# First batch's scores with tokens in the partitions, softmax along the free dimension, weights turned back by TensorE; both x halves from SyncE, activation table asked for early

## The chip, the cores and the metric

The kernel runs on one core of a Trainium2 chip. The metric is the device time of one execution in microseconds. Before the change three runs took 664.93, 666.25 and 666.53 us; the median, 666.25 us, is what the changed kernel is compared with. The trace comes from one more execution, whose own time was 665.42 us.

## The reference

There are 8 batches of 512 tokens in 8 heads of 64 numbers, and for each batch and head a state of 32 rows. The state reads the tokens and the tokens read the state (two softmax attentions over the same scores), and both results, laid side by side as 8 x 544 rows of 512, go through a two-layer network with an activation that is 0 below -1, the input above 1 and a parabola between.

```python
scores = scale * np.matmul(x, state.transpose(0, 1, 3, 2))     # B,H,512,32
a = softmax over the 32;   xread = np.matmul(a, state)
scores2 = scale * np.matmul(state, x.transpose(0, 1, 3, 2))    # B,H,32,512
a2 = softmax over the 512; sread = np.matmul(a2, x)
h = concatenate([xread, sread]).reshape(4352, 512) @ w_in      # 512 x 2048
g = np.where(h >= 1, h, np.where(h <= -1, 0.0, (h + 1) ** 2 / 4))
out = g @ w_out                                                 # 2048 x 512
```

All is float32. `x` is 26.7 times as large as drawn, so the softmaxes are far from flat.

## The kernel before, in words

Batches run one after the other, and each batch runs through 8 steps j, each with 256 of the 2048 columns of the hidden layer. Two heads and a state row block are joined into one contraction of 128 (4 pairs of heads with 32 state rows), so that the tokens' attention weights multiply a product of state and `w_in` directly: `sw` = state x `w_in` chunk, then `h` = `sw` x attention weights, then the activation, then `acc` += g x `w_out` chunk. Every large product is done as three float32r products of high and low parts (`ath`/`atl` for the weights of attention, `sw_h`/`sw_l`, `gh`/`gl`, `wo` high and low). Half of the work of VectorE (DVE) and ScalarE (ACT) is to make these parts.

The weights come in an encoded form: each chunk of `w_in` (`raw_i`) and of `w_out` (`raw_o`), 1 MB each, is decoded by three operations of 128x1024: `low` (on ACT or DVE), `high` (ACT) and `join` (DVE, L595); a `w_out` chunk is then also split (`part_high` on ACT, L602, `part_low` on DVE, L606). That decoding of 8 + 8 chunks happens once, during batch 0.

The start of the program and all of batch 0 are therefore ordered by a planner (`Plan`): each operation is given an engine, a cost, its prerequisites and the buffers that it takes and ends. The planner simulates a list schedule by rank (the length of the chain behind an operation, plus a hand-set `BIAS` for 19 operations), and emits the instructions in the order of that schedule. On PE (TensorE) and SP (SyncE, which issues the loads) the order is that of the listing. Where the plan leaves PE idle between the first scores and the first `g2`, `emit` fills in matmuls of the identity into a scratch tile (`warmed`, L198), one for each 0.34 us that the plan sees free. They do no work for the result.

Batch 0's attention, in the order of its steps, per q (the two heads of each pair, q = 0 and 1):

- `scores` (L253): state is the stationary operand (64x32), tokens move; the result `sc` has the 128 (pair, state row) in partitions and 512 tokens along the free dimension. For batch 0 it is done in two halves of 256 tokens, as the two halves of `xt` arrive. The first half of `xt` is issued by SP, the second by ACT.
- `turn` (L260): DVE transposes blocks of 32x32, so that the 32 state rows of a head lie along the free dimension (`z`); four half turns.
- `top1` (L271), `less1` (L275), `exp1` (L280, ACT), `sum1` (L284), `inv1` (L288, L289), `norm1` (L293): the softmax over 32.
- `back` (L300): DVE turns the weights back into `zt`; `high1` (L303, ACT) and `rest` (L306, DVE) split them into `ath` and `atl`.
- `top2` (L318, L319) and `exp2` (L322, ACT): the maximum and the exponential over the 512 tokens, from `sc` as it stands. `turn2` (`e2p`, L333), `keep_turned`, `read2` (`sr`, L350), `scale2`, `keep2` (`rt`) and `keep` finish the state's read.

PE's order is: fills, scores half 0, scores half 1, `sw` of chunk 0, h of step 0 (12 matmuls, L475 to L477), `sw` of chunk 1, then for each step j from 1: h of step j, `sw` of chunk j+1, the first half of `g2` of step j-1 (12 matmuls, L533 to L535), one item of the table `between`, the second half of `g2`. `e2p` of batch 0 is the item of j = 0. `sw`, `e2p`, `sr`, `sc` of batch 1 and `rt` share one pair of PSUM banks, `mm`, with one buffer; the scores of batch 0 and `acc` share `acc`, with four. `h` has two buffers, freed by `bound` (L487). The buffer of `xt` is single: batch 1's load, which stands on SP ahead of `raw_i` 3 and `raw_o` 2, waits until batch 0's scores are through.

After batch 0 (from `steps` on, L788) the order is written out by hand and nothing of the weights is left to decode.

Of the kernel before, what the change touches and what calls it, by code (L numbers as in the profile page):

```python
# [18 lines left out]
PAD = 120  # L19
BIAS = {('square', 0, 7): 4.9, ('high', 'o', 5): 4.6, ('wol', 7): -5.5, ('back', 0, 1): 2.8, ('atl', 1, 0): -6.5, ('w', 1): -2.8, ('swh', 0, 4): 4.5, ('wol', 5): 9.6, ('top2', 1, 1): 2.5, ('woh', 5): 4.1, ('swl', 1, 0): -0.5, ('swl', 0, 7): 2.1, ('gh', 0, 7): 0.6, ('low', 'i', 0): 2.6, ('wol', 6): 4.0, ('back', 1, 0): -2.1, ('turn', 0, 0, 1): -8.6, ('bound', 1, 0, 0): 3.3, ('high', 'o', 0): -4.3}  # L20

# [116 lines left out]
def state_exchange_moe(  # L138
# [39 lines left out]
    def ps_acc(name):  # L178
        return ps.tile([P, DM], F32, tag="acc", bufs=4, name=name)
# [45 lines left out]
    class Attention:  # L225
# [8 lines left out]

        def scores(self, half=None):
            b = self.b
            if half != 1:
                if b:
                    sc = ps_mm(f"sc{b}")
                    self.sc = [sc[:, hh] for hh in range(2)]  # L240
                else:
                    self.sc = [ps_acc(f"sc{b}_{hh}") for hh in range(2)]
                self.z = work.tile([P, 2, S], F32, tag="z", bufs=1, name=f"z{b}")
                self.m1 = small.tile([P, 2 * NM], F32, tag="m1", name=f"m1_{b}")
                self.s1 = small.tile([P, 2 * NM], F32, tag="s1", name=f"s1_{b}")
            for pr in range(NPR):
                for hh in range(2):
                    rows = slice(hh * 64, hh * 64 + 64)
                    o = self.sc[hh][pr * NS:(pr + 1) * NS]
                    m = self.xt[rows, :, pr]  # L250
                    if half is not None:
                        o, m = o[:, half * S // 2:(half + 1) * S // 2], m[:, half]
                    nc.tensor.matmul(o, lhsT=sb[rows, b, pr], rhs=m, start=True, stop=True)  # L253

        def tokens(self, half):
            return slice(None) if half is None else slice(half * S // 2, (half + 1) * S // 2)

        def turn(self, q, half=None):
            t = self.tokens(half)
            nc.vector.transpose(out=self.z[:, q, t], in_=self.sc[q][:, t])  # L260

# [4 lines left out]
        def top1(self, q, half=None):  # L266
            v, m, _ = self.parts(q)
            if half is not None:
                t = slice(half * NM // 2, (half + 1) * NM // 2)
                v, m = v[:, t], m[:, t]  # L270
            nc.vector.tensor_reduce(out=m, in_=v, op=ALU.max, axis=AX.X)  # L271

        def less1(self, q):
            v, m, _ = self.parts(q)
            nc.vector.tensor_tensor(  # L275
                out=v, in0=v, in1=m[:, :, None].broadcast_to([P, NM, NS]), op=ALU.subtract
            )
# [175 lines left out]
    class Hidden:  # L453
# [6 lines left out]

        def product(self, i):
# [5 lines left out]
            hp = ps_h(f"h{b}_{j}_{i}")  # L467
            for r in range(per):
                f = (2 * j + i) * per + r
                wh, wl = chunk[b, f // 2]  # L470
                sl = slice((f % 2) * P, (f % 2 + 1) * P)
                o = hp[:, r * n:(r + 1) * n]
                for k in range(nk):
# [4 lines left out]
            self.hs.append(hp)  # L478

# [160 lines left out]
    def att_start(b, half=None):  # L640
        if half != 1:
            atts[b] = Attention(b)
        atts[b].scores(half)

    def att_ops1(b):
# [27 lines left out]
    def att_ops2(b):  # L673
# [3 lines left out]
        for q in range(2):  # L677
            k = (b, q)
            take = [("tmp" if b == 0 else "e2", ("e2", b))] if q == 0 else []
            op(("top2",) + k, "DVE", 0.75, m("top2", q), [("sc", b) if b else ("sc", b, 1)] + [("top2", b, 0)] * q, take=take)  # L680
            op(("exp2",) + k, "ACT", 0.66, m("exp2", q), [("top2",) + k], ends=[("sc", b)])
# [20 lines left out]

    def product(i, b, j):
        if i == 0:
            hid[b, j] = Hidden(b, j)
        hid[b, j].product(i)

# [43 lines left out]
    op(("sc done", 0), "ACT", 0, lambda: None, [("exp2", 0, 0), ("exp2", 0, 1)])  # L751
    sw_ops(0, 0, 1)
    between = {
        0: lambda: tensor(("e2p", 0), 0.9, lambda: atts[0].turn2(), [("exp2", 0, 0), ("exp2", 0, 1)],
                          take=[("mm", ("e2p", 0))]),
        1: lambda: tensor(("sr", 0), 1.1, lambda: atts[0].read2(), [("kept", 0), ("dma", "xn", 0)],
                          take=[("mm", ("sr", 0))], ends=[("e2", 0), ("xn", 0)]),
        2: lambda: tensor(("sc", 1), 1.1, lambda: att_start(1), [("dma", "sb", 1), ("dma", "xt", 1)],
                          take=[("mm", ("sc", 1))], ends=[("xt", 1)]),
        3: lambda: tensor(("rt", 0), 0.3, lambda: atts[0].keep2(), [("rs", 0)], take=[("mm", ("rt", 0))]),  # L760
        4: lambda: tensor(("e2p", 1), 0.9, lambda: atts[1].turn2(), [("exp2", 1, 0), ("exp2", 1, 1)],
                          take=[("mm", ("e2p", 1))]),
        5: lambda: tensor(("sr", 1), 1.1, lambda: atts[1].read2(), [("kept", 1), ("dma", "xn", 1)],
                          take=[("mm", ("sr", 1))], ends=[("e2", 1), ("xn", 1)]),
        6: lambda: tensor(("rt", 1), 0.3, lambda: atts[1].keep2(), [("rs", 1)], take=[("mm", ("rt", 1))]),
    }
    for j in range(NJ):
        g1_ops(0, j)
        hidden_ops(0, j)
        if j + 1 < NC:  # L770
# [5 lines left out]
        if j == 2:  # L776
            att_ops1(1)
            att_ops2(1)
# [4 lines left out]
    with guard:  # L783
        plan.emit(warm, ("sc", 0, 0), ("g2", 0, 0, 0))

# [74 lines left out]
```

## Time and profile before

| | |
|---|---|
| median of three runs | 666.25 us |
| the profiled execution's own time | 665.42 us |
| its span, first to last instruction | 663.7 us |
| PE busy | 654.3 us (99%) |
| DVE busy | 340.0 us (51%) |
| ACT busy | 357.4 us (54%) |
| real h matmuls begin | 21.58 us |
| first `g2` matmul | 31.53 us |

PE's busy time counts the fills too, so that a busy PE in the first 28 us is not PE at useful work. The busy times of DVE and ACT are means over a stage in which they have no pause (the decoding of the weights in batch 0) and a long one in which they are half idle.

### The profile page before, as it was taken

The page shows a single profiled execution, that of the slowest core. Times are in us where ns is not written, and L with a number is a line of the kernel's source. Part 1 is how long each engine was busy: PE and PEld are TensorE (multiplying, and loading weights), DVE is VectorE, ACT ScalarE, POOL GpSimd, SP SyncE. Part 2 cuts the span into 40 slices and gives each one's busy share as a digit, 9 for nine tenths or more (in the row PEclk, how much of TensorE's full clock was granted, in tenths as well). Part 3 has the DMA queues.
Part 4 walks back from the last instruction along what each step waited for, and adds up shares of the span by engine and source line. Part 5 has one row for each costly group of instructions (what it writes and reads, how often), then busy time and mean ns, then how long its engine had stood idle before and what let it go on. Part 6 is the DMA issues. An engine that isn't in the chain of part 4 may idle for free.

```text
span 663.7 us, 10308 instructions
## 1 busy us (share of the span) xinstructions
PE 654.3 (99%) x4444; PEld 516.1 (78%) x4444; DVE 340.0 (51%) x489; ACT 357.4 (54%) x462; POOL 0.8 (0%) x7
## 2 busy tenths in 40 slices
PE   7999999999999999999999999999999999999997
PEld 6777777777777777777787777777788777778896
DVE  4999947623673338533573239433563343333531
ACT  4899847544564446544554447444653454454542
POOL 0000000000000000000000000000000000000000
PEclk9899999999999999999999999999999999999999
DMA  8896103010201003010301003010100001000101
GB/s 347 350 394 273 64 1 126 1 65 0 105 23 49 16 1 127 0 65 1 127 1 64 1 15 114 0 65 0 65 1 1 1 25 40 1 1 1 63 1 33
DMA packets 11085, 43.65 MB, mean 66 GB/s; under 512 B 1312, under 2 KB 1440, under 8 KB 7968
## 3 DMA queue, kind: packets, MB, share of 16 engines
q1 hardware_dynamic: 5952, 33.75, 13.4%
q10 hardware_dynamic: 5088, 9.24, 3.7%
q8 instruction: 35, 0.57, 0.4%
q14 instruction: 10, 0.08, 0.0%
HBM read 34.08 MB, written 8.91 MB: 65 GB/s over the span
## 4 chain that ended last, share of the span: by engine, by line
PE 92%; ACT 4%; DVE 2%; DMA 1%; issue 0%; ACTq 0%; SPq 0%
PE acc L533 19%; PE acc L534 18%; PE acc L535 18%; PE h L475 9%; PE h L476 9%; PE h L477 9%; PE sw L417 5%; DMA xt<-in_xt_dram 1%; PE sr L350 1%; PE sc L253 1%; PE e2p L333 1%; ACT u L481 1%; PE warmed L198 1%; ACT raw_i L587 1%; ACT gh L496 0%; ACT raw_o L587 0%
## 5 line engine op out<-in xcount | busy, mean ns | idle before, releaser
L533 PE MATMUL acc<-wo,gh 128*128 128x512 f32 x544 | 218.9, 402 | 0.0
L481 ACT ACTIVATE u<-h,half 128x512 f32<-128x512 f32 x136 | 93.6, 690 | 222.3 <-PE h L477 204.3
L534 PE MATMUL acc<-wo,gh 128*128 128x512 f32 x544 | 212.2, 390 | 0.0
L535 PE MATMUL acc<-wo,gl 128*128 128x512 f32 x544 | 212.2, 390 | 0.0
L487 DVE SCALAR_TENSOR_TENSOR u<-u,h 128x512 f32<-128x512 f32 x136 | 87.0, 681 | 206.4 <-ACT u L484 206.4
L533 PEld LDWEIGHTS acc<-wo,gh 128*128 128x128 f32 x544 | 102.1, 188 | 40.0 <-ACT u L481 12.8
L535 PEld LDWEIGHTS acc<-wo,gl 128*128 128x128 f32 x544 | 102.1, 188 | 22.6 <-issue 0.4
L534 PEld LDWEIGHTS acc<-wo,gh 128*128 128x128 f32 x544 | 102.3, 188 | 19.0
L501 DVE TENSOR_TENSOR gl<-u,gh 128x1024 fp32r<-128x1024 f32 x68 | 83.1, 1223 | 33.0 <-ACT gh L496 32.0
L496 ACT CAST gh<-u 128x1024 fp32r<-128x1024 f32 x68 | 71.6, 1052 | 50.8 <-DVE u L487 50.4
L484 ACT ACTIVATE u<-u 128x1024 f32<-128x1024 f32 x68 | 72.3, 1063 | 1.3
L417 PE MATMUL sw<-w,sb 64*32 64x256 f32 x1024 | 36.1, 384 | 2.2 <-DVE w L595 2.2
L417 PEld LDWEIGHTS sw<-w,sb 64*32 64x32 f32 x1024 | 15.1, 106 | 18.2 <-issue 9.5
L548 ACT COPY o<-acc 128x512 f32<-128x512 f32 x33 | 18.6, 585 | 9.1 <-PE acc L535 9.0
L476 PE MATMUL h<-ath,sw_0l 128*128 128x512 f32 x60 | 23.4, 389 | 0.0
L477 PE MATMUL h<-atl,sw_6h 128*128 128x512 f32 x60 | 23.4, 389 | 0.0
L475 PE MATMUL h<-ath,sw_0h 128*128 128x512 f32 x60 | 23.4, 392 | 0.0
L477 PE MATMUL h<-atl,sw_2h 128*128 128x512 f32 x60 | 23.4, 389 | 0.0
L477 PE MATMUL h<-atl,sw_0h 128*128 128x512 f32 x60 | 23.3, 389 | 0.0
L475 PE MATMUL h<-ath,sw_2h 128*128 128x512 f32 x60 | 23.3, 389 | 0.0
L476 PE MATMUL h<-ath,sw_2l 128*128 128x512 f32 x60 | 23.3, 389 | 0.0
L475 PE MATMUL h<-ath,sw_4h 128*128 128x512 f32 x60 | 23.3, 389 | 0.0
(173 smaller groups left out, 736.0 us busy)
## 6 DMA issues: line engine op xcount, KB each, us to landing
raw_i<-in_moe_w_in_dram SPq DMA_DIRECT2D x8, 1024.0 KB, 6.6
raw_o<-in_moe_w_out_dram SPq DMA_DIRECT2D x8, 1024.0 KB, 8.5
xn<-in_x_dram SPq DMA_DIRECT2D x8, 1024.0 KB, 5.5
out_dram<-o ACTq DMA_DIRECT2D x32, 256.0 KB, 2.0
xt<-in_xt_dram SPq DMA_DIRECT2D x15, 512.0 KB, 4.5
xt<-in_xt_dram ACTq DMA_DIRECT2D x1, 512.0 KB, 7.7
sb<-in_state_dram SPq DMA_DIRECT2D x1, 448.0 KB, 11.9
out_dram<-o SPq DMA_DIRECT2D x4, 64.0 KB, 1.7
```

The costliest lines, as they stand in the source:

```text
L417: nc.tensor.matmul(pt[pr * NS:(pr + 1) * NS, hh, i * CI:(i + 1) * CI], lhsT=sb[rows, b, pr], rhs=w32[c + i][rows, pr], start=True, stop=True,)
L475: nc.tensor.matmul(o, lhsT=wh[:, k, sl], rhs=ah[:, k], start=first, stop=False)
L476: nc.tensor.matmul(o, lhsT=wl[:, k, sl], rhs=ah[:, k], start=False, stop=False)
L477: nc.tensor.matmul(o, lhsT=wh[:, k, sl], rhs=al[:, k], start=False, stop=last)
L481: nc.scalar.activation(out=self.u[:, i], in_=self.hs[i], func=AF.Relu, scale=0.5, bias=half)
L484: nc.scalar.activation(out=self.u, in_=self.u, func=AF.Square)
L487: nc.vector.scalar_tensor_tensor(out=self.u[:, i], in0=self.u[:, i], scalar=1.0, in1=self.hs[i], op0=ALU.min, op1=ALU.max,)
L496: nc.scalar.copy(out=gh, in_=self.u)
L501: nc.vector.tensor_tensor(out=gl, in0=self.u, in1=gh.bitcast(F32), op=ALU.subtract)
L533: nc.tensor.matmul(a, lhsT=lh, rhs=oh, start=f == 0, stop=False)
L534: nc.tensor.matmul(a, lhsT=lh, rhs=ol, start=False, stop=False)
L535: nc.tensor.matmul(a, lhsT=ll, rhs=oh, start=False, stop=f == NF - 1)
```

## The change

The table `BIAS` is emptied. Both halves of batch 0's `xt` are issued by SP, one after the other. A first instruction on ACT copies one column of a scratch tile, so that the activation table is asked for before data arrive.

For batch 0, `scores_turned` computes the scores with tokens in the partitions: 64x128 of `xt` is the stationary operand and the state (64x32) moves, 16 products for each half of the tokens. `top1` and `less1` read that PSUM tile (`st`) directly, so the four half turns go. After `norm1` the weights are turned by TensorE (`turn_back`, 4 transposes of 128x128 for each q, into `zt` in `mm`) in place of DVE's `back`. `ath` and `atl` then read PSUM.

The old scores (`sc`), which `top2` and `exp2` need, are still computed, in one piece, on PE behind h of step 0; `top2` and `exp2` follow them. h of step 0 is cut in two by the contraction: the products with q = 0 of both row blocks, then those with q = 1. The items of `between` move one step on each (j = 1 to 7 in place of 0 to 6), and batch 1's attention follows its scores to j = 3.

```diff
-BIAS = {('square', 0, 7): 4.9, ('high', 'o', 5): 4.6, ...}
+BIAS = {}
@@ load_xt
-            (nc.scalar if i and b == 0 else nc.sync).dma_start(out=xt[:, i], in_=xt_in[b, i])
+            nc.sync.dma_start(out=xt[:, i], in_=xt_in[b, i])
@@ Attention
+        def scores_turned(self, half):
+            if half == 0:
+                self.st = [ps_acc(f"st{hh}") for hh in range(2)]
...
+            for t in range(2):
+                for pr in range(NPR):
+                    for hh in range(2):
+                        rows = slice(hh * 64, hh * 64 + 64)
+                        c0 = ((2 * half + t) * NPR + pr) * NS
+                        nc.tensor.matmul(
+                            self.st[hh][:, c0:c0 + NS], lhsT=self.xt[rows, half, pr, t * P:(t + 1) * P],
+                            rhs=sb[rows, self.b, pr], start=True, stop=True,
+                        )
+        def turn_back(self, q):
+            if q == 0:
+                self.zt = ps_mm(f"zt{self.b}")
+            for t in range(NT):
+                cols = slice(t * P, (t + 1) * P)
+                nc.tensor.transpose(out=self.zt[:, q, cols], in_=self.z[:, q, cols], identity=ident)
@@ top1, less1
+            if self.b == 0:
+                v = self.st[q].rearrange("p (j n) -> p j n", n=NS)
@@ att_ops1
-                    op(("turn",) + h, "DVE", 0.35, m("turn", q, half), [("sc", b, half)])
-                    op(("top1",) + h, "DVE", 0.35, m("top1", q, half), [("turn",) + h])
+                    op(("top1",) + h, "DVE", 0.35, m("top1", q, half), [("st", half)])
+            if b == 0:
+                tensor(("tz", q), 0.5, m("turn_back", q), [("norm1",) + k], take=[("mm", ("tz",))] if q == 0 else [])
+                op(("ath",) + k, "ACT", 0.48, m("high1", q), [("tz", q)], ends=[("tz",)])
+                op(("atl",) + k, "DVE", 0.62, m("rest", q), [("ath",) + k], ends=[("tz",)])
+                continue
@@ g1_ops
+        if j == 0:
+            for q in range(2):
+                for i in range(2):
+                    need = [(x, b, j) for x in ("swh", "swl")] + [(x, b, q) for x in ("ath", "atl")]
+                    tensor(("p", i, b, j) if q else ("p0", i), 0.72, lambda i=i, q=q: product(i, b, j, [q]), need,
+                           take=[] if q else [("h", ("h", i, b, j))], ends=[("wc", b, j)])
+            return
@@ listing
+    op(("table",), "ACT", 1.3, lambda: nc.scalar.copy(out=pad[:, :1], in_=half))
     tensor(("warm",), 4.5, lambda: warm(WARM))
     for side in range(2):
-        tensor(("sc", 0, side), 0.6, lambda side=side: att_start(0, side), [("dma", "xt", 0, side)],
-               ends=[("xt", 0)])
+        tensor(("st", side), 1.0, lambda side=side: att_start(0, side), [("dma", "xt", 0, side)])
+    sw_ops(0, 0, 1)
     att_ops1(0)
-    att_ops2(0)
-    sw_ops(0, 0, 1)
@@ for j in range(NJ)
         g1_ops(0, j)
         hidden_ops(0, j)
+        if j == 0:
+            tensor(("sc", 0), 1.1, lambda: atts[0].scores(), [("less1", 0, 0), ("less1", 0, 1)], ends=[("xt", 0)])
+            att_ops2(0)
```

## Rows read from the trace of the kernel before

**Rows 1.** The page: busy us of each engine; PE's busy tenths in 40 slices
```profile
PE 654.3 (99%) x4444; PEld 516.1 (78%) x4444; DVE 340.0 (51%) x489; ACT 357.4 (54%) x462; POOL 0.8 (0%) x7
...
PE   7999999999999999999999999999999999999997
```
**Rows 2.** Windows: stretch, length, busy PE, PEld, DVE, ACT, POOL; PEclk, DMA, GB/s
```profile
10.00:21.50 11.50, 9.34 (x80) 8.60 (x79) 11.36 (x25) 10.56 (x15) 0.00 (x0) 0.85 0.81 325
21.50:30.00 8.50, 7.96 (x58) 6.18 (x58) 7.48 (x12) 6.94 (x10) 0.00 (x0) 1.00 1.01 424
...
60.00:70.00 10.00, 10.00 (x62) 7.67 (x61) 9.96 (x15) 10.00 (x13) 0.00 (x0) 1.00 0.39 160
```
**Rows 3.** Windows of the fills alone (L198): PE and PEld busy us
```profile
21.50:30.00 8.50, 1.87 (x13) 1.40 (x12) 1.00 1.01 424
```
**Rows 4.** Timeline of DVE: start us, us, engine, line, operation, count [idle before]
```profile
9.76 0.78 DVE L260 STREAM_TRANSPOSE z<-sc 128x256 f32<-128x256 f32 x2 [1.15 <-PE sc L253]
10.47 0.70 DVE L271 TENSOR_REDUCE m<-z 128x8 f32<-128x256 f32 x2
11.09 1.28 DVE L275 TENSOR_TENSOR z<-z,m 128x512 f32<-128x512 f32 x2
12.29 0.68 DVE L318 TENSOR_REDUCE nm<-sc 128x1 f32<-128x512 f32 x1
...
16.09 1.22 DVE L595 SCALAR_TENSOR_TENSOR w<-raw_i 128x1024 int32<-128x1024 int32 x1
17.22 0.70 DVE L300 STREAM_TRANSPOSE zt<-z 128x512 f32<-128x512 f32 x1
17.85 0.65 DVE L318 TENSOR_REDUCE nm<-sc 128x1 f32<-128x512 f32 x1
...
21.00 1.22 DVE L595 SCALAR_TENSOR_TENSOR w<-raw_i 128x1024 int32<-128x1024 int32 x1
24.91 1.23 DVE L606 TENSOR_TENSOR wo<-wf,wo 128x1024 fp32r<-128x1024 f32 x1 [0.94 <-ACT wo L602]
26.65 0.69 DVE L574 TENSOR_SCALAR raw_o<-raw_o 128x1024 int32<-128x1024 uint32 x1
29.97 1.23 DVE L501 TENSOR_TENSOR gl<-u,gh 128x1024 fp32r<-128x1024 f32 x1
```
**Rows 5.** Timeline of PE up to its saturated stretch
```profile
6.01 1.11 PE L253 MATMUL sc<-xt,sb 64*32 64x256 f32 x16
...
8.98 0.67 PE L253 MATMUL sc<-xt,sb 64*32 64x256 f32 x16 [1.00 <-DMA xt<-in_xt_dram]
...
21.58 0.48 PE L475 MATMUL h<-ath,sw_0h 128*128 128x512 f32 x1
...
24.19 0.39 PE L477 MATMUL h<-atl,sw_0h 128*128 128x512 f32 x1
...
26.79 1.09 PE L333 MATMUL e2p<-ident,e 128*128 128x128 f32 x8 [0.54 <-DVE sw_1l L436]
27.72 0.39 PE L198 MATMUL warmed<-ident 128*128 128x128 f32 x2
27.99 0.50 PE L475 MATMUL h<-ath,sw_1h 128*128 128x512 f32 x1
...
31.53 0.50 PE L533 MATMUL acc<-wo,gh 128*128 128x512 f32 x1
```
**Rows 6.** Weight loads of fills and scores: ns min/median/max; starts; forms
```profile
L198 PEld LDWEIGHTS warmed<-ident x100: 186/192/338, 1.4 to 27.7; 128*128 128x128 f32 x100
...
L253 PEld LDWEIGHTS sc<-xt,sb x144: 102/106/151, 6.0 to 469.1; 64*32 64x32 f32 x144
```
**Rows 7.** DMA issues up to 1.5 us: KB each, us to landing
```profile
xt<-in_xt_dram ACTq DMA_DIRECT2D x1, 512.0 KB, 7.7
```
**Rows 8.** Timeline of ACT: the table's load
```profile
8.61 1.28 ACT L579 ACT_TABLE_LOAD   x1 [8.61 <-DMA raw_i<-in_moe_w_in_dram]
```
**Rows 9.** Timeline of SP's queue: the fourth chunk of w_in
```profile
22.28 0.33 SPq L567 DMA_DIRECT2D raw_i<-in_moe_w_in_dram  x1
```

More of the change, by code (lines that the diff above doesn't have):

```diff
@@ L19 @@
 PAD = 120
-BIAS = {('square', 0, 7): 4.9, ('high', 'o', 5): 4.6, ('wol', 7): -5.5, ('back', 0, 1): 2.8, ('atl', 1, 0): -6.5, ('w', 1): -2.8, ('swh', 0, 4): 4.5, ('wol', 5): 9.6, ('top2', 1, 1): 2.5, ('woh', 5): 4.1, ('swl', 1, 0): -0.5, ('swl', 0, 7): 2.1, ('gh', 0, 7): 0.6, ('low', 'i', 0): 2.6, ('wol', 6): 4.0, ('back', 1, 0): -2.1, ('turn', 0, 0, 1): -8.6, ('bound', 1, 0, 0): 3.3, ('high', 'o', 0): -4.3}
+BIAS = {}
 class Plan:
@@ L233, in __init__, with scores @@
             att_of[b] = (self.ath, self.atl)
-        def scores(self, half=None):
+        def scores(self):
             b = self.b
[L237 to L242, printed above, removed]
+            if b:
+                sc = ps_mm(f"sc{b}")
+                self.sc = [sc[:, hh] for hh in range(2)]
                 self.z = work.tile([P, 2, S], F32, tag="z", bufs=1, name=f"z{b}")
@@ L245, in scores @@
                 self.s1 = small.tile([P, 2 * NM], F32, tag="s1", name=f"s1_{b}")
+            else:
+                self.sc = [ps_acc(f"sc{b}_{hh}") for hh in range(2)]
             for pr in range(NPR):
@@ L248, in scores, with turn @@
                     rows = slice(hh * 64, hh * 64 + 64)
[L249 to L260, printed above, removed]
+                    nc.tensor.matmul(
+                        self.sc[hh][pr * NS:(pr + 1) * NS], lhsT=sb[rows, b, pr],
+                        rhs=self.xt[rows, :, pr], start=True, stop=True,
+                    )
+        def scores_turned(self, half):
+            if half == 0:
+                self.st = [ps_acc(f"st{hh}") for hh in range(2)]
+                self.z = work.tile([P, 2, S], F32, tag="z", bufs=1, name=f"z{self.b}")
+                self.m1 = small.tile([P, 2 * NM], F32, tag="m1", name=f"m1_{self.b}")
+                self.s1 = small.tile([P, 2 * NM], F32, tag="s1", name=f"s1_{self.b}")
+            for t in range(2):
[3 more added lines that the diff above has]
+                        c0 = ((2 * half + t) * NPR + pr) * NS
+                        nc.tensor.matmul(
+                            self.st[hh][:, c0:c0 + NS], lhsT=self.xt[rows, half, pr, t * P:(t + 1) * P],
+                            rhs=sb[rows, self.b, pr], start=True, stop=True,
+                        )
+        def turn_back(self, q):
[4 more added lines that the diff above has]
+                nc.tensor.transpose(out=self.zt[:, q, cols], in_=self.z[:, q, cols], identity=ident)
+        def turn(self, q):
+            nc.vector.transpose(out=self.z[:, q], in_=self.sc[q])
         def parts(self, q):
@@ L274, in less1 @@
             v, m, _ = self.parts(q)
+            src = v if self.b else self.st[q].rearrange("p (j n) -> p j n", n=NS)
             nc.vector.tensor_tensor(
-                out=v, in0=v, in1=m[:, :, None].broadcast_to([P, NM, NS]), op=ALU.subtract
+                out=v, in0=src, in1=m[:, :, None].broadcast_to([P, NM, NS]), op=ALU.subtract
             )
@@ L459, in __init__, with product @@
             self.hs = []
-        def product(self, i):
+        def product(self, i, ks=None):
             b, j = self.b, self.j
@@ L466, in product @@
             nk = ah.shape[1]
-            hp = ps_h(f"h{b}_{j}_{i}")
+            if not ks or 0 in ks:
+                self.hs.append(ps_h(f"h{b}_{j}_{i}"))
+            hp = self.hs[i]
             for r in range(per):
@@ L472, in product @@
                 o = hp[:, r * n:(r + 1) * n]
-                for k in range(nk):
+                for k in ks or range(nk):
                     first, last = k == 0, k == nk - 1
@@ L640, in att_start @@
     def att_start(b, half=None):
-        if half != 1:
+        if not half:
             atts[b] = Attention(b)
-        atts[b].scores(half)
+        if b:
+            atts[b].scores()
+        else:
+            atts[b].scores_turned(half)
     def att_ops1(b):
@@ L679, in att_ops2 @@
             take = [("tmp" if b == 0 else "e2", ("e2", b))] if q == 0 else []
-            op(("top2",) + k, "DVE", 0.75, m("top2", q), [("sc", b) if b else ("sc", b, 1)] + [("top2", b, 0)] * q, take=take)
+            op(("top2",) + k, "DVE", 0.75, m("top2", q), [("sc", b)] + [("top2", b, 0)] * q, take=take)
             op(("exp2",) + k, "ACT", 0.66, m("exp2", q), [("top2",) + k], ends=[("sc", b)])
@@ L701, in tensor, with product @@
         op(key, "PE", cost, f, after, take, ends)
-    def product(i, b, j):
-        if i == 0:
+    def product(i, b, j, ks=None):
+        if (b, j) not in hid:
             hid[b, j] = Hidden(b, j)
-        hid[b, j].product(i)
+        hid[b, j].product(i, ks)
     def sw_ops(b, c, n):
@@ L769, in state_exchange_moe @@
         hidden_ops(0, j)
+        if j == 0:
+            tensor(("sc", 0), 1.1, lambda: atts[0].scores(), [("less1", 0, 0), ("less1", 0, 1)], ends=[("xt", 0)])
+            att_ops2(0)
+            op(("sc done", 0), "ACT", 0, lambda: None, [("exp2", 0, 0), ("exp2", 0, 1)])
         if j + 1 < NC:
@@ L775, in state_exchange_moe @@
             between[j]()
-        if j == 2:
+        if j == 3:
             att_ops1(1)
@@ L783, in state_exchange_moe @@
     with guard:
-        plan.emit(warm, ("sc", 0, 0), ("g2", 0, 0, 0))
+        plan.emit(warm, ("st", 0), ("g2", 0, 0, 0))
     steps = [(b, j) for b in range(1, B + 1) for j in range(NJ if b < B else NJ // 2)]
```

16 lines of the change are left out of this document (7 added, 9 removed).

## The prediction

> **What bounds the kernel now.** The page comes first: PE is busy for 654.3 us of a span of 663.7, and in 40 slices it is full from the second to the last but one [rows 1]. So whatever the change does to DVE or ACT after the start is worth nothing by itself; time can only come from the first slices, where PE's work is not yet real. The windows say how far that reaches. From 10 to 21.5 us PE seems busy for 9.34 of 11.5 us, but no h matmul exists before 21.58 [rows 2, 5]; from 21.5 to 30 it has 0.54 us of idle time and 1.87 us of fills [rows 2, 3]. From 27.99 on the work is real and close [rows 5]. The engine that is full all the while is DVE: 11.36 of 11.5 us up to 21.5, and still 9.96 of 10 at 60 to 70 us, where PE is full too [rows 2]. The DVE timeline is read next, since it is the list of what PE waits for: turns, maxima and softmax from 9.76, `atl` of q = 1 ending where the next `join` starts (21.00), and `gl` of step 0 from 29.97 to 31.20, 0.33 us before the first `g2` at 31.53 [rows 4, 5]. Between 21.00 and 31.20 DVE pauses once, 0.94 us for `wo` [rows 4]. Reading: the first h waits for DVE's attention, the first `g2` for DVE's queue, and behind that PE never stops.
>
> **Scores the other way round.** Before, the second half's scores start at 8.98 and DVE reaches `less1` at 11.09 [rows 4, 5]. After, each half is 16 products with 64x128 of `xt` as weights; a float32 product shows as two instructions (16 for 8 products in rows 5), so 32 weight loads a half, 16 for each half of the rows. From 32 to 128 columns a load grows from 102 to 186 ns [rows 6], 0.875 ns a column, so I estimate 112 ns for 128 columns against 28 ns or so for a stream of 32. The load sets the pace. If the two row halves load side by side, a half costs 16 x 0.112 = 1.8 us; if not, 32 x (0.112 + 0.028) = 4.5 us; at the other end stands the price of the scores of today, 0.67 us [rows 5]. I take 1.8: today's 16 instructions begin 42 ns apart (0.67 / 16) where one load takes 102 [rows 5, 6], so loads of different tiles do lie side by side. The first half also runs before PE is at full speed: the same 16 instructions take 1.11 us at 6.01 and 0.67 at 8.98 [rows 5], so it costs up to 1.8 x 1.66 = 3.0, and I take 2.6. That gives 6.0 + 2.6 + 1.8 and 0.2 for the pipeline's end: 10.6 us. Two maxima of the second half, 0.62 us by their starts (10.47 to 11.09), bring `less1` to 11.2. **The four turns that go, 2 x 0.71 us, are thus paid back by slower scores**, and `less1` starts 0.1 us later than before. With the ends 0.67 and 4.5 a half it starts near 8.5 or near 16.
>
> **x half 1 from SP.** It landed 7.7 us after its issue on ACT [rows 7], and PE waited for it 1.0 us [rows 5]. On SP it lands ahead of the 3 MB of weights, some 3 us sooner, but PE is at half 0 until 8.6: the gain is hidden by the scores, 0.3 us at most. The 512 KB delay `raw_i` by what they no longer take beside it: nothing.
>
> **Softmax to h.** From 11.09 to 21.00 DVE spends 9.91 us [rows 4]. Two backs go, 0.63 each (17.22 to 17.85); two `top2` move behind h, 0.68 and 0.65 with a small operation each, 1.55 together. What is left is 7.1 us, and up to 0.6 for one `low` that the plan may now give DVE: `atl` ends between 18.3 and 18.9, I take 18.6 instead of 21.00. The turns by PE lie in a chain that is only a little longer: four of eight transposes of `e2p`, whose eight take 0.93 (26.79 to 27.72) [rows 5], so 0.5 us each q, and DVE has `join` and `swl` to do meanwhile. `zt` holds `mm` until `atl` is read; behind it stands `sw` of chunk 1, which comes after h in PE's order anyway. The first half of h runs while `atl` of q = 1 is made, so h ends 1.4 us (half of 24.42 - 21.58) after 18.6, at 20.3 with the waits, instead of 24.42.
>
> **h to the first g2.** Two bounds. The chain by its old length (24.42 to 31.53, 7.1 us) gives 27.4. DVE's queue gives more: from 21.00 to 31.20 it did 10.2 us, of which a `low` of `raw_o` 1 (0.60, 26.65) was not yet due and 0.94 was a wait; both `top2` (1.55) come in again. So 10.2 to 11.15, and with a third of the wait left, as ACT has the table's load off its path, 10.5. From 18.6: 29.1, and from the ends 28.5 and 30.0. The first `g2` follows 0.3 later as before: **29.4, 2.1 us earlier**. Splitting h and the short chain therefore give nothing beyond what DVE allows.
>
> **What goes into the saturated stretch.** `e2p` stood in the hole between h of steps 0 and 1 at 26.79 [rows 5]; as the item of j = 1 it stands between two `g2`, where every us of PE is the kernel's: its 0.93 comes to the sum in full, +0.9. `sc` in one piece (about 1.0) and `sw` 1 lie in the hole, which is longer than both. The items of j = 2 to 7 only change places. Gain: 2.1 - 0.9 = 1.2; 0.2 with DVE's late end, 1.8 with its early one.
>
> **Table and SP.** The load of 1.28 us at 8.61 [rows 8] goes under the first DMAs; ACT is not what DVE waits for there (scores end later), so I count 0.3 at most, inside the third above. SP's new wait: batch 1's `xt` cannot go before `sc` ends near 21.8, and `raw_i` 3, which went out at 22.28 [rows 9], stands behind it, some 1 us later, with PE 2 us earlier. Its product is needed after two more steps of PE; cover gone, the loss would be about 3 us, but two steps of 10 us cover it.
>
> The Trainium skill, ScalarE: Activation LUTs, section "Table sets: the hidden batching unit", says that copy and relu are fillers in every table set while exp has a set of its own. By that a copy as first instruction need not bring the exp set, and a second load might follow; the trace has one load, before a relu, and no second for exp, so the program's first choice held all it needs. With a second load the sum would be the rival below.
>
> **Sum.** 665.42 for the profiled execution less 1.2 is 664.2. The median of the runs shown is 0.8 higher, so 666.25 - 1.2, **665.0 us**, with 664.4 to 666.1 as this case's own range (gains of 1.8 and 0.2).
>
> **Rivals.**
> 1. *Scores or DVE's queue are cheaper than I take*: a half near 0.67 us puts `less1` at 8.5 to 9.3 and all behind it 2 us earlier, first `g2` at 27.4 (then the chain's bound too): 4.1 - 0.9 = 3.2, **663.0**. For it: DVE waits 1.15 us for scores even now [rows 4]; against it: 128 columns a load [rows 6]. 0.32.
> 2. *The emptied biases open holes*: with `mm` single, `sw`, the item of `between` and the splits wait on each other in each of seven steps, and DVE at 9.96 of 10 has nothing to spare. Holes of 0.3 us in each cost 2.1: **667.1**, and 665.7 with a third of it. Against it: 1.3 us less work on DVE (the backs). 0.11.
> 3. *The other side*: the row halves of `st` do not load side by side. Then a half costs 4.5 us, the first some 6 by its slow start, `st` ends near 14 to 16 and `atl` 3.5 to 5 us later than forecast: first `g2` at 32.9 to 34.4, 1.4 to 2.9 late, and 0.9 for `e2p`: 2.3 to 3.8 lost, **669.0**. It decides from `st` ending after 11.8 (no gain left) and is slower than measurable past 13.9. 0.06.
> 4. *A second table load*: 1.28 on ACT ahead of `exp1`, in DVE's chain: 665.0 + 1.3 = **666.3**. 0.03.
> 5. *The change doesn't do what it says*, because half 1's early landing and the split of h are hidden: that is inside the forecast, which counts them at nothing.
>
> **How the numbers follow.** Forecast 0.48, rivals 0.32, 0.11, 0.06, 0.03. About 0.3% (2.0 us) is what a measurement can tell: faster is below 664.25, slower above 668.25. Faster: rival 1 and 0.07 of the forecast, should its queue of DVE come out a us shorter, 0.39. Slower: rival 3's 0.05 and 0.04 of rival 2, 0.09. Same: 0.52. The range from 662.4 to 667.4 leaves out the lowest tenth (rival 1 at its far end) and rival 3 with part of rival 2.
>
> **What would show it.** `st` as 32 loads a half, 56 ns apart, ending near 10.6; `less1` at about 11.2, no L260 and no L300 for batch 0; `atl` ending near 18.6; h of step 0 ending near 20.3; a hole of about 3 us between h and `g2`; first `g2` near 29.4 and `e2p` behind its first half. Wrong: `st` ending before 9.5 or after 12, `gl` not the last before the first `g2`, or holes of PE after 32 us.

## The result, and the profile after

The changed kernel takes 667.36 us (median of 17 runs, 666.35 to 670.54). The kernel before, run beside it on the same chip, takes 665.51 us (17 runs, 664.93 to 666.89). The ratio is 1.0032, 95% interval 1.0023 to 1.0040: the change makes the kernel slower by 1.85 us. 665.0 was forecast, 0.5 faster than the before of these runs and 1.2 faster than the median that the forecast started from. The profiled execution took 667.26 us, its span is 665.5.

The page of the kernel after, busy time and PE's slices, beside [rows 1]:

```profile
PE 658.0 (99%) x4486; PEld 519.7 (78%) x4486; DVE 337.4 (51%) x483; ACT 357.7 (54%) x463; POOL 0.8 (0%) x7
...
PE   9999999999999999999999999999999999999997
```

Windows of the kernel after, as [rows 2] (stretch, length, busy us of PE, PEld, DVE, ACT, POOL, then granted clock, DMA share, GB/s):

```profile
10.00:21.50 11.50, 11.01 (x75) 9.46 (x74) 10.60 (x21) 7.21 (x9) 0.00 (x0) 0.77 0.98 410
21.50:30.00 8.50, 7.84 (x70) 5.57 (x69) 7.19 (x12) 7.58 (x11) 0.00 (x0) 1.00 0.55 198
60.00:70.00 10.00, 10.00 (x58) 7.51 (x57) 9.42 (x12) 9.80 (x15) 0.00 (x0) 1.00 0.63 261
```

DVE did get its time back: 10.60 us where it had 11.36 [rows 2], with room at 60 us too. ACT is down to 7.21 of 11.5 us there, so it waits. PE is fuller, and that is mostly fills at a lower clock (0.77, before 0.85). DVE is no longer what everything waits for.

PE's timeline of the kernel after, beside [rows 5]:

```profile
5.63 4.39 PE L265 MATMUL st<-sb,xt 64*128 64x32 f32 x64
9.95 5.49 PE L198 MATMUL warmed<-ident 128*128 128x128 f32 x24
15.37 0.66 PE L438 MATMUL sw<-w,sb 64*32 64x256 f32 x16
15.96 1.83 PE L198 MATMUL warmed<-ident 128*128 128x128 f32 x14
17.63 1.19 PE L275 MATMUL zt<-ident,z 128*128 128x128 f32 x8
...
19.49 0.50 PE L498 MATMUL h<-ath,sw_0h 128*128 128x512 f32 x1
...
20.71 0.50 PE L500 MATMUL h<-atl,sw_0h 128*128 128x512 f32 x1 [0.48 <-DVE atl L327]
...
22.89 0.39 PE L500 MATMUL h<-atl,sw_0h 128*128 128x512 f32 x1
...
27.99 0.47 PE L498 MATMUL h<-ath,sw_1h 128*128 128x512 f32 x1 [0.61 <-DVE u L509]
...
31.81 0.50 PE L555 MATMUL acc<-wo,gh 128*128 128x512 f32 x1
...
32.38 0.49 PE L557 MATMUL acc<-wo,gl 128*128 128x512 f32 x1
...
34.79 1.04 PE L354 MATMUL e2p<-ident,e 128*128 128x128 f32 x8
35.58 0.48 PE L555 MATMUL acc<-wo,gh 128*128 128x512 f32 x1
...
45.61 1.10 PE L371 MATMUL sr<-xn,e 128*32 128x64 f32 x64 [0.78 <-DVE sw_3l L457]
...
97.56 1.09 PE L438 MATMUL sw<-w,sb 64*32 64x256 f32 x32
```

The first h starts 2.1 us earlier than before (19.49 against 21.58), then half of it waits for `atl`; its last matmul starts 1.3 us earlier (22.89 against 24.19), and by h of step 1 all is gone: 27.99 in both. The first `g2` is 0.28 us late. Behind it come `e2p` between two `g2` and a hole of 0.78 us.

The fills tell of the clock: the 24 behind `st` take 229 ns each, the 14 from 15.96 on 131 ns. PE's windows of the kernel after (last columns granted clock, DMA share, GB/s) say it directly, 0.5 being 1.2 GHz and 1.0 being 2.4:

```profile
8.00:10.00 2.00, 2.00 (x27) 0.64 1.01 426
10.00:12.00 2.00, 2.00 (x11) 0.50 1.01 426
...
14.00:16.00 2.00, 2.00 (x24) 0.65 1.01 428
```

DVE's timeline of the kernel after, beside [rows 4]:

```profile
10.05 1.42 DVE L291 TENSOR_REDUCE m<-st 128x8 f32<-128x256 f32 x4 [9.15 <-PE st L265]
11.38 0.68 DVE L296 TENSOR_TENSOR z<-st,m 128x512 f32<-128x512 f32 x1
11.98 0.68 DVE L596 TENSOR_SCALAR raw_i<-raw_i 128x1024 int32<-128x1024 uint32 x1
...
13.18 1.22 DVE L617 SCALAR_TENSOR_TENSOR w<-raw_i 128x1024 int32<-128x1024 int32 x1
...
17.96 1.22 DVE L617 SCALAR_TENSOR_TENSOR w<-raw_i 128x1024 int32<-128x1024 int32 x1
19.96 1.29 DVE L327 TENSOR_TENSOR atl<-zt,ath 128x512 fp32r<-128x512 f32 x2 [0.78 <-ACT ath L324]
...
26.03 1.22 DVE L617 SCALAR_TENSOR_TENSOR w<-raw_i 128x1024 int32<-128x1024 int32 x1
27.17 0.68 DVE L509 SCALAR_TENSOR_TENSOR u<-u,h 128x512 f32<-128x512 f32 x1
...
31.10 1.22 DVE L523 TENSOR_TENSOR gl<-u,gh 128x1024 fp32r<-128x1024 f32 x1
```

And ACT's, where the table's load of [rows 8] now stands at the start, with no second one, and `ath` stands behind a decoding of 1.16 us:

```profile
1.24 1.28 ACT L781 ACT_TABLE_LOAD   x1 [1.24 <-DVE half L190]
...
17.78 1.16 ACT L609 ACTIVATE raw_o<-raw_o 128x1024 f32<-128x1024 f32 x1
18.86 1.07 ACT L324 CAST ath<-zt 128x512 fp32r<-128x512 f32 x2
...
24.52 1.19 ACT L609 ACTIVATE raw_i<-raw_i 128x1024 f32<-128x1024 f32 x1
25.61 1.04 ACT L506 ACTIVATE u<-u 128x1024 f32<-128x1024 f32 x1
```

These rows show where the 1.3 us by which h ended earlier went. Ahead of `square` (L506) ACT does a decoding of 1.19 us, so that `square` starts at 25.61, against 25.82 before; ahead of `bound` (L509) DVE does a `join`, so that `bound` starts at 27.17, against 27.25. h of step 1 waits for `bound`, which frees its buffer.

**The ledger of the two traces.** First `g2`: +0.28 (31.81 less 31.53). From the first `g2` to the first `sw` behind 90 us: 65.75 against 64.20 us, +1.55. In the kernel before, that `sw` is

```profile
95.73 1.09 PE L417 MATMUL sw<-w,sb 64*32 64x256 f32 x32
```

Of the 1.55, PE's idle time between 35 and 62 us is 0.78 against 0.14, +0.64, and the remaining 0.9 is as much as `e2p` takes. Together +1.83, the span's +1.8. This says where the time lies, not that each part could be had back by itself (see e7).

### The profile page after: what moved, and what is told of

Same layout as the page of the kernel before. It is cut to its first block, busy times and chain, and to the rows that moved or that the text cites. A ratio compares the mean times of both kernels' runs of the same rounds, so it can differ in the third digit from the quotient of the medians.

```text
span 665.5 us, 10389 instructions
## 1 busy us (share of the span) xinstructions
PE 658.0 (99%) x4486; PEld 519.7 (78%) x4486; DVE 337.4 (51%) x483; ACT 357.7 (54%) x463; POOL 0.8 (0%) x7
## 4 chain that ended last, share of the span: by engine, by line
PE 94%; ACT 3%; DVE 1%; DMA 0%; issue 0%; POOL 0%; SPq 0%; ACTq 0%; POOLq 0%
PE acc L555 19%; PE acc L557 18%; PE acc L556 18%; PE h L498 9%; PE h L500 9%; PE h L499 9%; PE sw L438 5%; PE warmed L198 1%; PE sr L371 1%; PE sc L248 1%; PE e2p L354 1%; PE st L265 1%; ACT u L503 0%; ACT raw_i L609 0%; ACT wo L624 0%; ACT raw_o L609 0%
## 5 line engine op out<-in xcount | busy, mean ns | idle before, releaser
L509 DVE SCALAR_TENSOR_TENSOR u<-u,h 128x512 f32<-128x512 f32 x136 | 87.0, 680 | 206.3 <-ACT u L506 206.3
L506 ACT ACTIVATE u<-u 128x1024 f32<-128x1024 f32 x68 | 72.2, 1062 | 1.3
L570 ACT COPY o<-acc 128x512 f32<-128x512 f32 x33 | 18.6, 585 | 9.2 <-PE acc L557 9.1
## 6 DMA issues: line engine op xcount, KB each, us to landing
raw_o<-in_moe_w_out_dram SPq DMA_DIRECT2D x8, 1024.0 KB, 10.8
sb<-in_state_dram SPq DMA_DIRECT2D x1, 448.0 KB, 12.5
```

The costliest lines, as they stand in the source:

```text
L506: nc.scalar.activation(out=self.u, in_=self.u, func=AF.Square)
L509: nc.vector.scalar_tensor_tensor(out=self.u[:, i], in0=self.u[:, i], scalar=1.0, in1=self.hs[i], op0=ALU.min, op1=ALU.max,)
```

## The experiments

Theory before the first run: the start was slower than forecast because of the order in which the short softmax, the decoding and the turns were laid out, and because of the clock; `e2p` costs what was forecast. Rivals: the emptied biases alone; the deferral; `st` itself. Changes of one line stand as diffs; where a kernel's order was laid out again, its biases were chosen anew.

**e1: the kernel before with its biases emptied.**

```
-BIAS = {('square', 0, 7): 4.9, ('high', 'o', 5): 4.6, ...}
+BIAS = {}
```

> The kernel before with its 19 biases emptied and nothing else changed. Theory A (a good part of the loss is the emptied biases, which leave decoding that is not due in the queues of DVE and ACT ahead of what PE waits for): about 1 us slower than before, 666.2 to 667.0, and the first g2 0.7 to 1.3 us later than at 31.53. Rival B (the loss is all in the new scores, the fills at half clock and the turns by PE): no difference, within 0.4 us of before. Rival C (biases don't matter at the first g2 but open holes later): first g2 unchanged, PE idle of 0.7 us or more after 32 us.

Measured: 666.11 us, ratio 1.0004 (0.9994 to 1.0013). No difference is shown, and PE idles only 0.06 us between 35 and 62 us. Emptied biases do not by themselves open the hole at 45 us; what they cost inside the changed kernel is not separated by this run. Its profiled execution has the first `g2` at 32.46, 0.93 later than before, as theory A has it, but that was the slowest of the eleven (667.23), in which the second half's scores waited 2.12 us for the DMA instead of 1.00.

**e2, e3: on the old scores, both x halves from SP, then the early table as well.**

```
-            (nc.scalar if i and b == 0 else nc.sync).dma_start(out=xt[:, i], in_=xt_in[b, i])
+            nc.sync.dma_start(out=xt[:, i], in_=xt_in[b, i])
...
+    op(("table",), "ACT", 1.3, lambda: nc.scalar.copy(out=pad[:, :1], in_=half))     # e3
```

> The kernel before, biases kept, with both halves of the first batch's xt issued by SP, and nothing else. Theory A (in the kernel before the second half's landing holds the scores, so this part alone is a gain that slower scores hide in the changed kernel): second scores end near 7.7 in place of 9.65, DVE's softmax begins about 1.5 us earlier, first g2 0.5 to 1.5 us earlier, 664.3 to 665.2. Rival B (DVE's and ACT's queue of decoding is what holds the first g2, as raw_i 0 still lands at 8.6): under 0.4 us.

> The same as the run with both halves by SP, plus the copy on ACT that loads the table at the start. Theory A: ACT is then free 1.28 us earlier at 8.5, decoding follows the softmax more closely: another 0.3 to 0.8 us, 663.6 to 664.8 in all. Rival B: the load was hidden in the wait for scores, no further gain over the run without it (under 0.3 us).

Measured: e2 664.65, ratio 0.9987 (0.9977 to 0.9997); e3 664.49, ratio 0.9982 (0.9973 to 0.9991). PE's timeline of e2 answers to [rows 5]: the second half's scores no longer wait for the DMA and start at 6.54, not 8.98.

```profile
5.29 0.66 PE L253 MATMUL sc<-xt,sb 64*32 64x256 f32 x16
...
6.54 0.99 PE L253 MATMUL sc<-xt,sb 64*32 64x256 f32 x16
...
29.61 0.50 PE L533 MATMUL acc<-wo,gh 128*128 128x512 f32 x1
```

The DMA's part of the change is a gain of about 0.9 us without the rest. The table's 0.16 is too small to tell.

**e11: the changed kernel with half 1 back on ACT**, the line of e2 the other way round.

> The changed kernel with one part undone: half 1 of x is issued by ACT again. Prediction's view (SP for half 1 is hidden behind the slow first half of st): within 0.5 us of the changed kernel's 667.4; st of half 1 still follows half 0 with no wait above 0.3. Rival (half 1 from ACT lands near 9 us, as before the change, and st of half 1 waits up to 1 us for it as the scores did): 0.5 to 1.2 us slower, 667.9 to 668.6, with the wait in the trace.

Measured: 669.75, ratio to before 1.0060 (1.0047 to 1.0074). Both expectations missed: that one line is worth 2.4 us in the changed kernel. PE's timeline of e11:

```profile
5.76 1.98 PE L265 MATMUL st<-sb,xt 64*128 64x32 f32 x32
8.93 3.63 PE L265 MATMUL st<-sb,xt 64*128 64x32 f32 x32 [1.19 <-DMA xt<-in_xt_dram]
12.49 4.45 PE L198 MATMUL warmed<-ident 128*128 128x128 f32 x24
```

`st` ends near 12.5, not 9.95. Of those 2.5 us 1.19 is the wait, and 1.2 is that the second half takes 3.63 where the changed kernel's takes 2.4 (4.39 less the 1.98 of a first half): the granted clock was 0.71 in 8 to 10 us and 0.50 in 10 to 12. A wait inside `st` is paid twice, as a wait and as more of `st` at half clock.

**e4, e12: the planner is told that a half of `st` takes 2.2 us; in e4 with 19 new biases, in e12 with none.**

```
-        tensor(("st", side), 1.0, lambda side=side: att_start(0, side), [("dma", "xt", 0, side)])
+        tensor(("st", side), 2.2, lambda side=side: att_start(0, side), [("dma", "xt", 0, side)])
```

> The changed kernel with the planner's cost of a half's scores at 2.2 us, as measured, in place of 1.0, and with biases chosen anew for this plan (so fewer fills and another order on DVE and ACT; the work is the same). Theory A (order): the first g2 comes 1.0 to 1.8 us earlier than at 31.81 and no hole follows, 665.3 to 666.3, 1 to 2 us faster than the changed kernel but still not faster than before by more than 0.3 us, as e2p stays in the saturated stretch. Rival B (the scores and turns themselves are what costs): under 0.5 us of gain, 667.0 or more.

> The changed kernel with one number altered: the planner counts 2.2 us for each half of st instead of 1.0, biases still empty. Theory (the order before the first g2 was laid out for scores that end 2 us too early, and this is what cost the forecast's 2.1 us): atl of q = 1 ends before 20.5, first g2 between 29.4 and 31, time 666.0 to 667.0. Rival (the order suffers from the emptied biases, not from the price of st): first g2 at 31.5 or later, 667.2 or more. The 2x2 of e4 with this one tells how much of e4's 1.3 us is the price and how much the biases.

Measured: e4 666.03, ratio 1.0009 (0.9995 to 1.0023); e12 666.80, ratio 1.0025 (1.0013 to 1.0037). By the medians the right price alone is worth 0.6 us, the new biases beside it another 0.8; the intervals of neighbours among the three kernels touch or overlap, so only the two together are near to being shown. e12's time is as expected, but its first `g2` missed: 33.06 in the profiled execution, whose clock was at 0.5 from about 9 to 19.3. PE's timeline of e4, whose clock was at 1.0 from 4.27 on:

```profile
5.21 3.76 PE L265 MATMUL st<-sb,xt 64*128 64x32 f32 x64
...
18.46 0.66 PE L275 MATMUL zt<-ident,z 128*128 128x128 f32 x4 [0.56 <-DVE atl L327]
18.87 0.47 PE L498 MATMUL h<-ath,sw_0h 128*128 128x512 f32 x1
...
29.34 0.50 PE L555 MATMUL acc<-wo,gh 128*128 128x512 f32 x1
```

This is the forecast's first `g2` (29.4), and yet the kernel is no faster than before: from there to the first `sw` behind 90 us it takes 65.67 us, 0.9 of it `e2p` and 0.6 holes. e4's executions also price the clock: five with a mean granted clock of 1.000 took 665.0 to 665.2, four with 0.994 to 0.996 took 666.0 to 666.3. In the changed kernel two with 0.999 took 666.4 and twelve with 0.994 to 0.997 took 667.2 to 667.8. So about 1.0 us hangs on whether the clock falls behind `st`. The executions left over, two of e4 at 669.1 and 669.2 and three of the changed kernel at 670.2 to 670.5, are of a third kind, which e7 and e8 show. The kernel before has its own share of the slower clock: in the runs beside these experiments its executions with 0.999 took 664.7 to 665.4, its medians 665.5 to 665.6. Compared at 0.999, the changed kernel is still about 1.4 us slower.

**e5, e9, e6: the deferral and `st`, each with and without.** e5 is e3 with the second softmax and `e2p` moved behind h as in the change; e9 is e4 without that move; e6 is e3 with neither, but with h split by halves as in the change. The diff is e5's; the items of `between` behind `e2p` move by one step with it. In e9 `e2p` and the rest go back, and `sc` is made right behind `st`. All three have biases of their own.

```
-            op(("top2",) + k, "DVE", 0.75, m("top2", q), [("sc", b) if b else ("sc", b, 1)] + [("top2", b, 0)] * q, take=take)
+            op(("top2",) + k, "DVE", 0.75, m("top2", q), ([("sc", b)] if b else [("sc", b, 1), ("p", 1, 0, 0)]) + [("top2", b, 0)] * q, take=take)
...
-        0: lambda: tensor(("e2p", 0), 0.9, lambda: atts[0].turn2(), [("exp2", 0, 0), ("exp2", 0, 1)],
+        1: lambda: tensor(("e2p", 0), 0.9, lambda: atts[0].turn2(), [("exp2", 0, 0), ("exp2", 0, 1)],
```

> One part of the change alone: the kernel before with both x halves by SP and the early table (664.5 us), old scores and turns by DVE kept, but top2 and exp2 of batch 0 wait for h of step 0, and e2p and the items behind it stand one step later, as in the changed kernel; biases chosen anew. sc is not computed twice. Theory A (deferral gives back more than it takes: two top2 and two exp2 come into the stretch before the first g2, and e2p into the saturated stretch): h ends up to 0.5 us earlier, the first g2 is no earlier than 29.4, and the time is 0.9 to 1.5 us above the run without the deferral, 665.4 to 666.0. Rival B (the scores with tokens in partitions are what costs, the deferral is free): 664.3 to 664.8.

> The other way round: the kernel before with both x halves by SP, the early table and the split of h of step 0 by q, with nothing deferred and the old scores; biases chosen anew. Theory A (DVE's and ACT's queues bound the first g2, not h): the gain over the same without the split is small, 0 to 0.5 us: 664.0 to 664.5, which would be the fastest version so far. Rival B (h's start bounds): 1 us or more, below 663.6.

> The changed kernel with its short chain given up: st, the turns by TensorE, the x halves by SP, the early table and the split h stay, the planner is told 2.2 us for st, but sc is made right behind st and top2, exp2 and e2p of batch 0 stand before the first g2 again, as before the change; the seven biases are searched anew. Theory (the deferral moves 0.9 us of e2p and the second softmax into the saturated stretch, and st buys nothing over the old scores): no e2p between two g2, first g2 near 30 us, 0.5 to 1 us below e4's 666.0, and 0.7 to 1.3 above e6's 663.9, that is 664.6 to 665.5. Rival (the deferral pays for itself by an earlier first g2): at or above 666.0. Second rival (st is worth as much as the old scores): within 0.4 of 663.9.

Measured, medians in us and ratios to before:

| | old scores | `st` |
|---|---|---|
| deferred | e5: 664.73, 0.9994 (0.9983 to 1.0004) | e4: 666.03, 1.0009 (0.9995 to 1.0023) |
| not deferred | e6: 663.87, 0.9980 (0.9971 to 0.9988) | e9: 664.84, 0.9983 (0.9974 to 0.9991) |

By the medians the deferral costs 1.2 on `st`, and there the two intervals lie apart. On the old scores it is between 0.2 and 0.9: 0.9 is against e6, which has the split of h besides, 0.2 against e3, which has neither, and the intervals overlap; e5's time lies in the range of its rival B, by which the deferral is free on the old scores. `st` costs 1.3 and 1.0 by the medians, but 1.0 and 0.2 by the ratios, whose intervals overlap in both rows: that `st` costs something is likely and not shown. e6 and e3 (0.9982) can't be told apart either, so what the split of h gives is open. No pair is in favour of `st` or of the deferral. In e9 `e2p` is back in the hole and the first `g2` is 1.5 us later than in e4 (whose profiled execution had the better clock, as e9's was at 0.5 for 3.4 us behind `st`), but the first `sw` behind 90 us is 0.4 us earlier: 63.80 us from the first `g2`, with no hole at all from 35 to 95 us. PE's timeline of e9:

```profile
26.40 1.09 PE L354 MATMUL e2p<-ident,e 128*128 128x128 f32 x8 [0.79 <-DVE sw_1l L457]
...
30.80 0.50 PE L555 MATMUL acc<-wo,gh 128*128 128x512 f32 x1
```

DVE's timeline of e9 shows how little the deferral had cleared away: one `top2` stands where the changed kernel's DVE idled for 0.78 us, and `atl` starts at 20.19 against 19.96 (e9's order and clock differ in other things too).

```profile
19.33 0.68 DVE L339 TENSOR_REDUCE nm<-sc 128x1 f32<-128x512 f32 x1
...
20.19 1.29 DVE L327 TENSOR_TENSOR atl<-zt,ath 128x512 fp32r<-128x512 f32 x2
```

**e7: the changed kernel with `e2p` of batch 0 made twice** (its transposes are issued a second time into the same place).

> The changed kernel with batch 0's e2p (8 transposes by PE, the item of j = 1) done twice over, writing the same values; the result is the same. Theory A (e2p stands in the saturated stretch, where all of PE's time counts): 0.8 to 1.0 us slower than the changed kernel (667.36), 668.2 to 668.4, with the second 8 in line right behind the first. Rival B (there is slack around it): under 0.3 us.

Measured: 668.93 by the median, but no execution lies near it. Three took 667.19 to 667.68, with a mean granted clock of 0.993 or 0.994, and three 670.18 to 670.31. The changed kernel's executions stand in the same places, twelve at 667.2 to 667.8 and three at 670.2 to 670.5. Like against like, with few executions, the second `e2p` costs about 0.2 us at most, which is rival B, although it takes 0.87 us of PE (1.91 against 1.04). The profiled execution is one of the second three, in which `st` took 7.04 us:

```profile
6.01 7.04 PE L265 MATMUL st<-sb,xt 64*128 64x32 f32 x64
...
37.76 1.91 PE L355 MATMUL e2p<-ident,e 128*128 128x128 f32 x16
...
48.60 1.10 PE L372 MATMUL sr<-xn,e 128*32 128x64 f32 x64
```

The hole has swallowed it: `sr` starts without a wait, 13.82 us behind the first `g2` (34.78), where the changed kernel takes 13.80 with its wait of 0.78 for `sw_3l`. To the first `sw` behind 90 us it is 65.76 us, against 65.75. So up to `sr` it is the queues behind `sw_3l` that set the pace in the changed kernel, not PE. Where PE does not wait, `e2p` costs nearly its length: e12 has no hole there and takes 65.02 us for the same stretch, 0.82 more than the kernel before.

**e8: the changed kernel with half as many fills.**

```
-                    n = int((begun[k] - idle) / 0.34)
+                    n = int((begun[k] - idle) / 0.68)
```

> The changed kernel with half as many fills (one for each 0.68 us that the plan sees free). In the changed kernel's trace 24 fill instructions run at 0.50 of the clock until 15.37 and 14 more until 17.6, where join of chunk 0 was through at 14.4 and norm1 of q = 0 at 16.8. Theory A (overrunning fills hold sw of chunk 0 by 0.9 us and the turns by 0.8): first h 0.3 to 1.0 us earlier, the time 0.2 to 1.0 us less, 666.4 to 667.1. Rival B (ACT's decoding stands between the turns and h anyway): within 0.2 us of 667.36. Rival C (PE falls to half clock for longer without the fills): slower, 668 or more.

Measured: 669.12, 1.76 us slower, ratio to before 1.0059 (1.0047 to 1.0071), as rival C has it: with half of the fills the clock was worse, four executions at 0.987 to 0.992 where the changed kernel has 0.994 to 0.999. Whether the fills are also in the way of `sw` and the turns can't be read from it. In the profiled execution `st` takes 7.04 us as in e7, and matmuls run at half speed until about 24.4.

**e10: e3 with fills of 32 columns for 128**, with the same weight loads.

```
-            nc.tensor.matmul(warmed[:, :P], lhsT=ident, rhs=ident, start=True, stop=True)
+            nc.tensor.matmul(warmed[:, :NS], lhsT=ident, rhs=ident[:, :NS], start=True, stop=True)
```

> The kernel before with both x halves by SP and the table early (e3), whose fills of TensorE multiply 32 columns instead of 128 with the same load of weights. Theory (the granted clock fell behind st because st, like these fills, is loads of weights with short streams): the granted clock is 0.5 in part of 8 to 20 us or rises later, and the time is 0.7 us or more above e3's 664.5. Rival (the clock's fall in the changed kernel has to do with the fills' number or their place, not with the length of the streams): clock as in e3, time within 0.4 of 664.5.

Measured: 670.44 (670.13 to 670.96), 5.95 us above e3, ratio to before 1.0067 (1.0055 to 1.0079). PE's timeline of e10:

```profile
8.92 10.45 PE L198 MATMUL warmed<-ident 128*128 128x32 f32 x48
19.29 1.11 PE L417 MATMUL sw<-w,sb 64*32 64x256 f32 x16
...
24.19 0.77 PE L475 MATMUL h<-ath,sw_0h 128*128 128x512 f32 x1
...
27.75 0.41 PE L477 MATMUL h<-atl,sw_0h 128*128 128x512 f32 x1
28.00 0.40 PE L475 MATMUL h<-ath,sw_0h 128*128 128x512 f32 x1
```

PE was full from 1.45 to 24.2 us and stayed at the lower of its two levels: `sw` takes 1.11 where it takes 0.66 in the changed kernel, and h's matmuls start 0.43 us apart up to 27.75 and 0.23 to 0.25 apart from there on. `st` is of the same make, loads of 128 columns with streams of 32, and the changed kernel's clock fell in the middle of it; in e4's profiled execution the same `st` kept the higher level, so this is what ran when the clock fell, not a rule for when it does. (The page shows 1.00 in a stretch ahead of the first recorded change of the clock; there the lengths of like instructions are what to read.)

## Why the prediction was wrong

**Held.** The new scores cost what was worked out: 64 loads in 3.76 us at the full clock (e4), 59 ns each where 56 was estimated, side by side; `st` ended at 9.95 against 10.6 and `less1` started at 11.38 against 11.2. Rivals 1 and 3, a cheaper or a dearer `st`, are out. There is no second table load, so rival 4 is out too, and no engine waits for a DMA between 14 and 60 us, so SP's new wait did no harm, though `raw_i` 3 went out at 25.33, 3 us later than before and not 1. Two of the three signs of being wrong came true: `gl` was not the last thing ahead of the first `g2`, and PE has a hole after 32 us.

**Right in size by luck: "h to the first g2".** From `atl`'s end to the first `g2` 10.8 us were forecast, and 10.56 measured (21.25 to 31.81). But the first `g2` does not wait for `gl`: in the changed kernel `gl` ends at 32.32, and its first use is the third product, at 32.38. PE reaches the first `g2` by its own order, behind h of step 1 and the next `sw`; h of step 1 starts when `bound` has freed its buffer, and the first `g2` follows its start by 3.5 to 3.9 us in both kernels and in e4, e9 and e12. The 0.33 us between `gl`'s end and the first `g2` in the kernel before, from which the step was built, was no wait either: that `g2` reads `gh` and follows h of step 1 there too.

**Failed: "Softmax to h", the term "`atl` ends between 18.3 and 18.9".** It ended at 21.25, 2.65 us late, about as late as before. The step took DVE's list and struck out what the change removes, as if DVE stayed the engine that all waits for. By the rows after, three things filled the gap: the second `join` (1.14 at 17.96), which is not needed before h; the wait of 0.78 for `ath`; and `low` (0.60, of which half was in the 18.6). With `less1` 0.18 late these are 2.4 of the 2.65. The wait is the telling one. Turned by PE, the weights go through DVE, PE, ACT and DVE again, and each of these hands is behind something: PE behind 24 fills at half clock, so that `sw` 0 starts at 15.37 although `join` was done at 14.40; ACT behind `high` of raw_o until 18.86; DVE until the second of the two `ath` is through (19.93), although h of q = 0 starts behind the first, at 19.49, for which the record shows no reason; and in e4 and e12 the second turn behind `atl` of the first half (0.56 and 0.51). "A chain only a little longer" was the sentence that failed. Even in e4, with the full clock and an order laid out for it, `atl` ended at 20.46.

**Unforeseen: the clock.** Rows of before showed it at 0.5 for a while (0.85 in [rows 2]), and the prediction took it into the first half of `st` only. It fell at 8.58, in `st`, for 6.8 us; by the executions of e4 and of the changed kernel that costs about 1.0 us. It acts through the same chain, so it is a part of `atl`'s 2.65 and does not come on top. In the difference to the kernel before, whose clock was at 0.5 for about 3.4 us (0.85 over 11.5 us), an estimate is 0.5 us (1.85 less the 1.4 at like clock). And where it rises late, `st` pays 7.04 for 3.76 us, where the two halves of the old scores pay 1.11 for 0.67 each.

**Mis-sized: "x half 1 from SP", 0.3 us at most.** Its cover, half 0 of `st` until 8.6, ended at 7.7 (e11). The line is worth 0.9 on the old scores and 2.4 here; without it the changed kernel is 4.2 us slower than before (e11).

**Mis-sized: "What goes into the saturated stretch", +0.9, and rival 2, the holes.** The stretch is not saturated everywhere. There is one hole of 0.78 us for `sw_3l` ahead of `sr`, not one in each step, and behind the first `g2` the change loses 1.55 us where 0.9 was forecast. A second `e2p` in front of the hole costs nothing (e7), so by the same reading `e2p`'s own 0.9 is not a cost by itself either as long as the hole stands behind it; no run takes it away alone. What opens the hole stays open. Emptied biases alone do not (e1); emptied biases with the deferral do not when the planner has the right price of `st` (e12, idle 0.00 us from 35 to 62), nor does the deferral on the old scores (e5, 0.00). e8 and e11, whose order behind the first `g2` is the changed kernel's, have it at the same place with 0.79 and 0.78 us. So it hangs on the order and the timing laid out, not on the biases or the deferral by themselves.

The sum by these terms: -1.2 forecast, +2.65 for `atl`, -0.24 for the stretch behind it, +0.64 for the hole: +1.85, which is what was measured. This is the ledger again and has to close; it says where the forecast was off, and the causes are as strong as said at each term.

**The best version** is e6: the old scores, the x halves from SP, the table early, h split by halves and biases of its own, 663.87 us, 1.3 us faster than the kernel before by the ratio (0.9980, 0.9971 to 0.9988), 1.6 by the medians, and 3.5 faster than the changed one. e3, which has neither the split nor new biases, is within the noise of it.

## What to carry to other kernels

Taking work off the engine that bounds a stretch is worth only as much as the next chain leaves: write that chain out hand by hand, with what stands in front of each hand on its own engine, before subtracting. Work moved out of a stretch that has holes into one that is full costs its time as far as PE sets the pace there (0.82 in e12), and nothing where PE waits for another queue further on (e7); e9 gave up 1.5 us at the start and still won. When two events stand 0.3 us apart, look which one the later instruction reads before calling it a wait. Ask of each line of a change that "does nothing" what its cover is and when that cover ends; here the one line that was counted at nothing was the only part that was shown to gain.

## What the runs showed of the hardware

- Loads of 128 float32 columns for row halves lie side by side: 59 ns apart (3.76 us for 64), though the trace gives a single one 182 ns or more.
- In e10 TensorE was busy without a pause from 1.45 us, with loads followed by streams of 32 columns, and its granted clock was at the lower of its two levels until about 27.8 us; in e3, which has 128 columns in the same places, like instructions have their short lengths from 5.62 us on (`scores` 0.66 us, 1.11 in e10).
- The clock's course differs between executions of one kernel: three of 17 of the changed kernel took 670.2 to 670.5 us, like the profiled ones of e7 and e8, in which `st` ran at half speed throughout.
